# Attention into a dense mixture of experts on one core: joint outputs later in their slot, hi parts of weights and operands on other engines around the last pass, six buffers for raw weights

## The chip, the core and the metric

The kernel runs on one core of a Trainium2 chip. The core has five engines that each work through a queue of their own, in program order, and wait for each other by semaphores: TensorE (PE in the profile, its weight loads PEld), VectorE (DVE), ScalarE (ACT), GpSimd (POOL), and SyncE (SP), which here only issues DMAs. Matmul results land in PSUM, everything else lives in SBUF. The metric is the device time of one launch in microseconds, the median of several runs.

## The reference

The attention part takes q, k, v of shape (4, 8, 576, 64), a memory M_prev (4, 8, 64, 64) with its norm z_prev, and a gate beta per head. The second part runs every token through all four experts.

```python
scores = (q @ k^T) / 8, causal mask; a = softmax(scores); local = a @ v
q_p = where(q > 0, q, exp(q) - 1) + 1
mem_out = (q_p @ M_prev) / (q_p . z_prev + 1e-6)
attn = g * mem_out + (1 - g) * local              # g = sigmoid(beta), per head
x = attn as (2304, 512);  p = probs / sum(probs)
out = sum over e of p[:, e] * (relu(x @ w1[e]) @ w2[e])   # w1 (4,512,1024), w2 (4,1024,512)
```

All inputs and the output are float32.

## The kernel before

**Precision.** Each float32 operand of a large matmul is split into hi and lo: hi is the operand written as fp32r, lo is the operand minus hi. A product is then three matmuls, hi·hi, hi·lo and lo·hi, summed in PSUM. So every weight tile and every activation costs one instruction that writes hi and one that subtracts it to give lo.

**The expert passes.** The 2304 tokens are 18 tiles of 128. Twelve of them form six groups of two tiles (`GROUPS`), six form the last pass (`TAIL`). A phase is one half of one expert: `mm1` makes four blocks of h (`h`, line 848; relu to `hh` on ScalarE, line 857; `hl` on VectorE, line 858), `mm2` multiplies them by w2 (`y`, line 878) and VectorE adds them to `acc` (line 894). A group takes eight phases. Neighbouring groups overlap: phases 0 to 28 hold one or two groups each, phases 25 to 28 only group 5. The last pass is phases 29 to 36 (`tail_phase`). It forms x·w1 by seven block products instead of eight; its operands (`A11`, `S1`, `S2`, `A12`, `S3`, `S4`, `A22`, each 128x768) are made once by `x_ops` from the attention's output `xt`, as eleven pieces: four sums or differences (line 991) and seven `put`s (hi on line 983, lo on line 984). They are dealt out during phases 27 and 28, one after every third part of a phase. Its weights are made by `wt_prep`: four sums of blocks `tsum`, hi `wth` on ScalarE, lo `wtl`. For phase 29 the sums and lo are on VectorE.

**The weights.** `w_dma` loads a raw tile of 128x512 (`stg`, 256 KB) on SP's queue, from a pool of `NSTG` = 4 buffers; `w_prep` makes hi and lo. GpSimd always makes lo (line 247). Hi is on ScalarE (line 244) for w1 until phase 26 and for w2 in the first phases, otherwise on GpSimd (line 246). A new load is issued once a preparation has freed a buffer. w2 of a phase is prepared during that phase's `mm1`, w1 of the next phase during `mm2`; each of the hi and lo buffers for the weights exists once.

**The attention beside it.** The attention is cut into tasks (one pair of heads, two or three query tiles), and tasks into slots. Each step of a task has a slot and a place in it, written in the table `PR` as [slot, place]; steps are sorted by both, and then dealt out between the parts of the expert phases by a running sum of estimated costs (`target`). Twelve tasks are "joint": both heads in one slot, four slots to a task. A joint task's steps on TensorE are `tq`, `tk`, `tp` (transposes of q, k and of phi(q); results split to hi and lo by ScalarE and VectorE, `split_q`, lines 365 to 372), `sp` (scores, line 479), `pt` (transposed probabilities) and `o` (output, lines 551 and 555). `tq`, `tk`, `tp` and `o` share two PSUM buffers ("to"), so each of them waits until the one two places back has been read out.

`j_o`, the joint output, stands at slot +4, place -0.2; the scores `j_qk` of the task that runs in that slot stand at place 0, and the transposes of probabilities at place 7. The read-out of `tp` (`qpa`, `qpb` on VectorE) stands one slot earlier at place 4.5.

```python
ev(i + PR["jo"][0], PR["jo"][1], lambda i=i: j_o(i), 6 * mm(GW) + 4 * mm(P))
act = (kind == "1" or i < START[1]) and i < PH0 - PR["ahead"] and not pool   # PH0 = 29, ahead = 2
```

Of the kernel before, what the change touches and what calls it, by code (L numbers as in the profile page):

```python
# [10 lines left out]
AF = mybir.ActivationFunctionType  # L11
# [11 lines left out]
PR = {  # L23
    "phi1": [-5, 1],
    "phi2": [-5, 7],
    "phi3": [-4, 7],
    "trq": [-3, 6.5],
    "trk": [-4, -0.5],
    "v": -2,
    "trqp": [1, 2.5],  # L30
    "qk": 0,
# [5 lines left out]
    "jn": [1, -0.45],  # L37
    "jp": [2, 7],
    "jlo": 9,
    "jo": [4, -0.2],  # L40
    "wpe": 1500,
    "wvec": 400,
    "frac": 0.97,
# [13 lines left out]
def tile_attention_moe(  # L57
# [13 lines left out]
    nc = tc.nc  # L71
# [38 lines left out]
    START = [g // 2 * NPH + (PR["x"] if g % 2 else 0) for g in range(NG)]  # L110
    PH0 = START[-1] + NPH
# [20 lines left out]
    def f(ap):  # L132
        return ap.bitcast(F32)

    def rows(c):
        return min(P, S - c * P)
# [61 lines left out]
        for kind in "12"  # L198
        for fc in (range(HF) if i < PH0 else (0, 2, 1, 3))
    ]  # L200
    NSTG = 4
    wpos = {"dma": 0, "prep": 0, "due": 0}
    stg = {}

    def w_dma():
        j = wpos["dma"]
        if j >= len(wseq):
            return
        wpos["dma"] += 1
        i, kind, fc = wseq[j]  # L210
        e, hf = halves[i]
        f0 = (hf * HF + fc) * P
        t = sp.tile([P, DM], F32, tag="stg", name=f"stg{j}", bufs=NSTG)
        stg[j] = t
        if kind == "1":
            nc.sync.dma_start(
                out=t.rearrange("p (c f) -> p c f", c=NKD),
                in_=w1[e, :, f0 : f0 + P].rearrange("(c p) f -> p c f", p=P),
            )
        else:  # L220
            nc.sync.dma_start(out=t, in_=w2[e, f0 : f0 + P, :])

    def w_more():

        while wpos["due"]:
            wpos["due"] -= 1
            w_dma()

    def w_prep(i, kind, pool=False):

        act = (kind == "1" or i < START[1]) and i < PH0 - PR["ahead"] and not pool
        j = wpos["prep"]
        if j >= len(wseq) or wseq[j][0] != i or wseq[j][1] != kind:
            return
        w_more()
        wpos["prep"] += 1
        fc = wseq[j][2]
        t = stg.pop(j)
        hi, lo = (w1s if kind == "1" else w2s)[fc]
        if kind == "1":  # L240
            hi = hi.rearrange("p c f -> p (c f)")
            lo = lo.rearrange("p c f -> p (c f)")
        if act:
            nc.scalar.activation(hi, t, AF.Copy)  # L244
        else:
            nc.gpsimd.tensor_scalar(hi, t, 1.0, 1.0, ALU.mult, ALU.mult)  # L246
        nc.gpsimd.tensor_tensor(lo, t, f(hi), ALU.subtract)  # L247
        wpos["due"] += 1
# [566 lines left out]
    def pcol(pieces):  # L815
        b, c = pieces[0]
        return 4 * b + c if c < 4 else 4 * B + b // 2
# [47 lines left out]
    def mm2(i, g, tt, after):  # L865
        e = halves[i][0]
        pieces = GROUPS[g][tt]
        pe = pn[:, pcol(pieces), e : e + 1]
        t0 = (g % 2) * GW + tt * P
        tk = slice(t0, t0 + P)  # L870
        pt = []

        def part(fc):
            if fc == 0:
                pt.append(ps.tile([P, 512], F32, tag="moe", name=f"y{i}_{g}_{tt}", bufs=3))
            wh, wl = w2s[fc]
            for z, (h_, w_) in enumerate(((hh, wh), (hh, wl), (hl, wh))):
                nc.tensor.matmul(  # L878
                    pt[0],
                    lhsT=h_[fc][:, tk],  # L880
                    rhs=w_,
                    start=(fc == 0 and z == 0),
                    stop=(fc == HF - 1 and z == 2),
                )
            if fc == HF - 1:
                fin()
                after()

        def fin():
            if i == START[g]:  # L890
                acc[g, tt] = sp.tile([P, DM], F32, tag="acc", name=f"acc{g}_{tt}", bufs=4)
                nc.vector.tensor_scalar(acc[g, tt], pt[0], pe, None, ALU.mult)
            else:
                nc.vector.scalar_tensor_tensor(  # L894
                    acc[g, tt], pt[0], pe, acc[g, tt], ALU.mult, ALU.add
                )
            if i == START[g] + NPH - 1:
                o0 = 0
                for b, c in pieces:
                    r0, m = b * S + c * P, rows(c)  # L900
                    nc.sync.dma_start(out=out[r0 : r0 + m, :], in_=acc[g, tt][o0 : o0 + m])
                    o0 += m

        return [lambda c=c: part(c) for c in range(HF)]

    def phase_parts(i):
        gs = [g for g in range(NG) if START[g] <= i < START[g] + NPH]
        c0 = min(g % 2 for g in gs) * GW
        cols = slice(c0, c0 + len(gs) * GW)
        out_ = []  # L910
        for fc in range(HF):
            for p_ in mm1(i, fc, cols, lambda: w_prep(i, "2")):
                out_.append((3 * mm(len(gs) * GW), p_))
        if i + 1 in START:
            out_.append((0.0, START.index(i + 1)))
        nt = 2 * len(gs)

        def after():
            if i + 1 == PH0:
                wt_prep(PH0)  # L920
            else:
                for _ in range(HF // nt):
                    w_prep(i + 1, "1")

        for g in gs:
            for tt in range(2):
                for p_ in mm2(i, g, tt, after):
                    out_.append((3 * mm(DM), p_))
        return out_
# [43 lines left out]
    def a_blk(i, k):  # L973
        return xt[:, 2 * k : 2 * k + 2, i * TB : (i + 1) * TB]

    def x_ops():

        X, s_ = tail["x"], tail["s"]
        s3 = tail["r"][:, 0:2]

        def put(n, src, eng):
            hi, lo = X[n]
            nc.scalar.activation(hi, src, AF.Copy)
            eng.tensor_tensor(lo, src, f(hi), ALU.subtract)

        def plain(n, i, k):
            return [lambda: put(n, a_blk(i, k), nc.vector)]

        def summed(n, eng, dst, a, b, op):
            return [  # L990
                lambda: eng.tensor_tensor(dst, a, b, op),
                lambda: put(n, dst, eng),
            ]

        return (
            plain("A11", 0, 0)
            + summed("S1", nc.vector, s_, a_blk(1, 0), a_blk(1, 1), ALU.add)
            + summed("S2", nc.vector, s_, s_, a_blk(0, 0), ALU.subtract)
            + summed("S4", nc.vector, s_, a_blk(0, 1), s_, ALU.subtract)
            + summed("S3", nc.vector, s3, a_blk(0, 0), a_blk(1, 0), ALU.subtract)  # L1000
            + plain("A12", 0, 1)
            + plain("A22", 1, 1)
        )

    def wt_prep(i):

        j = wpos["prep"]
        if j >= len(wseq) or wseq[j][0] != i or wseq[j][1] != "1":
            return
        w_more()  # L1010
        wpos["prep"] += 2
        t1, t2 = stg.pop(j), stg.pop(j + 1)
        hi, lo = tail["w"][wseq[j][2]]
        t = tail["t"]
        b11, b21, b12, b22 = t1[:, 0:GW], t1[:, GW:], t2[:, 0:GW], t2[:, GW:]
        t1 = t1.rearrange("p (n w) -> p n w", w=GW)
        gp = (nc.vector if i == PH0 else nc.gpsimd).tensor_tensor
        gp(t[:, 0], b12, b11, ALU.subtract)
        gp(t[:, 1], b22, t[:, 0], ALU.subtract)
        gp(t[:, 2], b22, b12, ALU.subtract)  # L1020
        gp(t[:, 3], b21, t[:, 1], ALU.subtract)
        nc.scalar.activation(hi[:, 0:2], t1, AF.Copy)
        nc.scalar.activation(hi[:, 2], b22, AF.Copy)
        nc.scalar.activation(hi[:, 3:7], t, AF.Copy)
        gp(lo[:, 0:2], t1, f(hi[:, 0:2]), ALU.subtract)
        nc.vector.tensor_tensor(lo[:, 2], b22, f(hi[:, 2]), ALU.subtract)
        nc.vector.tensor_tensor(lo[:, 3:7], t, f(hi[:, 3:7]), ALU.subtract)
        wpos["due"] += 2
# [86 lines left out]
    def tail_phase(i):  # L1115
        for p in range(2):
            tail_mm1(i, p)
            for _ in range(2):
                w_prep(i, "2")
        for t in range(0, NTL, 2):  # L1120
            tail_mm2(i, (t, t + 1))
            if t < 4:
                wt_prep(i + 1)


    def first_run():
# [20 lines left out]
        for h0, h1 in ((0, 2), (2, 4), (4, 8)):  # L1147
# [3 lines left out]
            if h0 == 0:  # L1151
# [4 lines left out]
                )  # L1156
        for _ in range(NSTG):
            w_dma()
# [310 lines left out]
```

## Time and profile before

| What | Value |
|---|---|
| Median of 3 runs | 1083.83 us (1081.46 to 1086.19) |
| The profiled execution's own time | 1078.98 us |
| Its span, first to last instruction | 1077.2 us |
| TensorE busy | 1011.6 us, 94% |
| VectorE busy | 736.7 us, 68% |
| GpSimd busy | 628.9 us, 58% |
| ScalarE busy | 504.2 us, 47% |
| Mean granted TensorE clock | 0.980 of 2.4 GHz |

TensorE is busy for most of the span, so its idle time and the time in which it runs at less than full clock are what can be read as loss. A row of "windows" cuts the span into stretches and gives the busy time of each engine in each; a row of "waits" gives an engine's idle time by what ended it; the timeline lists instructions with the idle time of their engine just before them in brackets.

### The profile page before, as it was taken

The page shows a single profiled execution, that of the slowest core. Times are in us where ns is not written, and L with a number is a line of the kernel's source. Part 1 is how long each engine was busy: PE and PEld are TensorE (multiplying, and loading weights), DVE is VectorE, ACT ScalarE, POOL GpSimd, SP SyncE. Part 2 cuts the span into 40 slices and gives each one's busy share as a digit, 9 for nine tenths or more (in the row PEclk, how much of TensorE's full clock was granted, in tenths as well). Part 3 has the DMA queues.
Part 4 walks back from the last instruction along what each step waited for, and adds up shares of the span by engine and source line. Part 5 has one row for each costly group of instructions (what it writes and reads, how often), then busy time and mean ns, then how long its engine had stood idle before and what let it go on. Part 6 is the DMA issues. An engine that isn't in the chain of part 4 may idle for free.

```text
span 1077.2 us, 16403 instructions
## 1 busy us (share of the span) xinstructions
PE 1011.6 (94%) x5312; PEld 857.6 (80%) x5312; DVE 736.7 (68%) x1708; ACT 504.2 (47%) x1193; POOL 628.9 (58%) x669
## 2 busy tenths in 40 slices
PE   5887889988999999999999999999978999999998
PEld 3776777777888888878888878778866888999887
DVE  5777767777777788778777878877375555445453
ACT  4666655554555555555555555545223333333231
POOL 4767567555556655565555654647895644555540
PEclk8999899999999999999999999999988999999999
DMA  5557444453445444354444434423434312222211
GB/s 135 132 152 181 118 130 121 120 142 96 109 115 136 103 134 109 97 146 115 116 105 121 121 106 108 115 85 110 146 99 137 88 54 61 62 70 69 78 40 58
DMA packets 205957, 116.87 MB, mean 108 GB/s; under 512 B 100272, under 2 KB 181680, under 8 KB 205872
## 3 DMA queue, kind: packets, MB, share of 16 engines
q1 hardware_dynamic: 205200, 115.56, 39.7%
q8 instruction: 42, 0.69, 0.3%
q14 instruction: 43, 0.35, 0.1%
q10 hardware_dynamic: 672, 0.27, 0.1%
HBM read 100.57 MB, written 4.72 MB: 98 GB/s over the span
## 4 chain that ended last, share of the span: by engine, by line
PE 72%; DVE 12%; POOL 6%; issue 4%; ACT 3%; DMA 2%; SPq 1%; POOLq 0%; DVEq 0%; ACTq 0%
PE h L848 18%; PE y L878 17%; PE yt L1094 12%; PE tc_1X L1043 3%; PE o L722 3%; PE pt L357 3%; PE sp L611 3%; PE tc_0X L1043 3%; POOL w2l L247 3%; DMA stg<-in_moe_w_dram 2%; POOL w1l L247 2%; PE tc_1Y L1043 1%; PE tc_0Y L1043 1%; POOL w2h L246 1%; DVE hl L858 1%
## 5 line engine op out<-in xcount | busy, mean ns | idle before, releaser
L247 POOL TENSOR_TENSOR w1l<-stg,w1h 128x512 fp32r<-128x512 f32 x116 | 153.3, 1328 | 241.1 <-ACT w1h L244 194.7
L247 POOL TENSOR_TENSOR w2l<-stg,w2h 128x512 fp32r<-128x512 f32 x148 | 196.2, 1325 | 18.0 <-ACT w2h L244 6.1
L848 PE MATMUL h<-xh,w1h 128*128 128x512 f32 (+1 forms) x464 | 176.1, 379 | 0.4 <-DVE hl L858 0.4
L848 PE MATMUL h<-xh,w1l 128*128 128x512 f32 (+1 forms) x464 | 165.2, 356 | 1.8 <-POOL w1l L247 1.8
L878 PE MATMUL y<-w2h,hh 128*128 128x512 f32 x384 | 165.1, 430 | 1.6 <-DVE hl L858 1.0
L848 PE MATMUL h<-xl,w1h 128*128 128x512 f32 (+1 forms) x464 | 164.2, 354 | 0.0
L878 PE MATMUL y<-w2l,hh 128*128 128x512 f32 x384 | 155.9, 406 | 7.2 <-POOL w2l L247 5.6
L878 PE MATMUL y<-w2h,hl 128*128 128x512 f32 x384 | 154.9, 403 | 0.2 <-DVE hl L858 0.2
L858 DVE SCALAR_TENSOR_TENSOR hl<-h,hh 128x512 fp32r<-128x512 f32 (+1 forms) x116 | 69.1, 596 | 59.6 <-ACT hh L857 58.6
L857 ACT ACTIVATE hh<-h 128x512 fp32r<-128x512 f32 (+1 forms) x116 | 60.8, 524 | 92.8 <-PE h L848 91.6
L246 POOL TENSOR_SCALAR w2h<-stg 128x512 fp32r<-128x512 f32 x132 | 88.1, 667 | 19.9 <-DMA stg<-in_moe_w_dram 12.7
L848 PEld LDWEIGHTS h<-xh,w1l 128*128 128x128 f32 x464 | 87.5, 189 | 15.1 <-POOL w1l L247 2.2
L894 DVE SCALAR_TENSOR_TENSOR acc<-y,pn,acc 128x512 f32<-128x512 f32 x84 | 62.8, 748 | 51.7 <-PE y L878 50.9
L848 PEld LDWEIGHTS h<-xh,w1h 128*128 128x128 f32 x464 | 87.8, 189 | 9.3 <-DVE hl L858 0.6
L848 PEld LDWEIGHTS h<-xl,w1h 128*128 128x128 f32 x464 | 88.2, 190 | 7.7
L878 PEld LDWEIGHTS y<-w2l,hh 128*128 128x128 f32 x384 | 74.9, 195 | 21.9 <-POOL w2l L247 12.1
L658 ACT ACTIVATE pth<-pt 128x384 fp32r<-128x384 f32 (+3 forms) x128 | 50.4, 421 | 85.4 <-PE pt L357 84.7
L878 PEld LDWEIGHTS y<-w2h,hl 128*128 128x128 f32 x384 | 74.5, 194 | 17.1 <-DVE hl L858 0.5
L878 PEld LDWEIGHTS y<-w2h,hh 128*128 128x128 f32 x384 | 74.8, 195 | 14.3 <-POOL w2h L246 1.8
L1107 DVE SCALAR_TENSOR_TENSOR xt<-yt,pn,xt 128x512 f32<-128x512 f32 x42 | 31.5, 751 | 61.1 <-PE yt L1094 61.1
L357 PE MATMUL pt<-ident,s 128*128 128x128 f32 (+1 forms) x376 | 62.0, 276 | 10.3 <-DVE ptl L660 8.3
L357 PEld LDWEIGHTS pt<-ident,s 128*128 128x128 f32 (+1 forms) x376 | 45.4, 139 | 29.6 <-issue 10.9
(297 smaller groups left out, 2440.6 us busy)
## 6 DMA issues: line engine op xcount, KB each, us to landing
stg<-in_moe_w_dram SPq DMA_DIRECT2D x296, 256.0 KB, 2.8
natall<-in_k_dram SPq DMA_DIRECT2D x34, 128.0 KB, 2.7
natall<-in_v_dram SPq DMA_DIRECT2D x32, 128.0 KB, 3.0
natall<-in_q_dram SPq DMA_DIRECT2D x60, 64.0 KB, 2.6
out_dram<-acc SPq DMA_DIRECT2D x12, 256.0 KB, 2.1
kha<-kha SPq DMA_DIRECT2D x16, 128.0 KB, 2.4
khb<-khb SPq DMA_DIRECT2D x16, 128.0 KB, 2.3
natall<-in_k_dram SPq DMA_DIRECT2D x28, 64.0 KB, 2.6
```

What stands on the lines that cost most here:

```text
L246: nc.gpsimd.tensor_scalar(hi, t, 1.0, 1.0, ALU.mult, ALU.mult)
L247: nc.gpsimd.tensor_tensor(lo, t, f(hi), ALU.subtract)
L357: nc.tensor.transpose(dst, src, ident[0:n, 0:n])
L611: nc.tensor.matmul(pt[:, 0 : b_ - a], lhsT=q_, rhs=qk[k_][:, a:b_], start=y == 0, stop=y == len(pairs) - 1,)
L658: nc.scalar.activation(dh, src, AF.Copy)
L848: nc.tensor.matmul(pt[0][:, cols], lhsT=w_[:, c], rhs=x_[:, c, cols], start=(c == 0 and z == 0), stop=(c == NKD - 1 and z == 2),)
L857: nc.scalar.activation(h_, pt[0][:, cols], AF.Relu)
L858: nc.vector.scalar_tensor_tensor(l_, pt[0][:, cols], 0.0, f(h_), ALU.max, ALU.subtract)
L878: nc.tensor.matmul(pt[0], lhsT=h_[fc][:, tk], rhs=w_, start=(fc == 0 and z == 0), stop=(fc == HF - 1 and z == 2),)
L894: nc.vector.scalar_tensor_tensor(acc[g, tt], pt[0], pe, acc[g, tt], ALU.mult, ALU.add)
L1043: nc.tensor.matmul(bank[b][:, 0:TB], lhsT=w_[:, n, cs], rhs=x_[:, c], start=first and c == 0 and z == 0, stop=c == 1 and z == 2, skip_grou ...
L1094: nc.tensor.matmul(o, lhsT=h_[fc][:, tk], rhs=w_, start=(z == 0 and fc == p and y == 0), stop=(z == 1 and fc == p + 2 and y == 2),)
```

## The change

Five edits:

1. The joint output `j_o` moves from place -0.2 to place 3 of its slot.
2. Raw weights have six buffers instead of four.
3. For phases 27 and 28, hi of w1 and w2 is made by ScalarE and no longer by GpSimd.
4. In phase 28 the first `wt_prep` for phase 29 is called after the first block of the first token tile of `mm2`, not after its last; the second follows at the end of the first tile, not of the second.
5. In `x_ops`, hi of the last pass's operands is copied by VectorE (`tensor_copy`) and no longer by ScalarE.

```diff
-    "jo": [4, -0.2],
+    "jo": [4, 3],
...
-    NSTG = 4
+    NSTG = 6
...
-        act = (kind == "1" or i < START[1]) and i < PH0 - PR["ahead"] and not pool
+        act = (kind == "1" or i < START[1] or PH0 - PR["ahead"] <= i < PH0) and not pool
...
+            if fc == 0 and i + 1 == PH0 and tt == 0:
+                wt_prep(PH0)
             if fc == HF - 1:
                 fin()
...
         def put(n, src, eng):
             hi, lo = X[n]
-            nc.scalar.activation(hi, src, AF.Copy)
+            eng.tensor_copy(hi, src)
             eng.tensor_tensor(lo, src, f(hi), ALU.subtract)
```

TensorE's queue around the third joint output (`o` is the output, `sp` the scores of the next task, `y` the experts' second product). Before:

```order
L878 MATMUL y_0_0_1334<-w2h_123,hl_111 128x512
L551 MATMUL o_1342<-qpa_86,ms_0_509 128x256
L555 MATMUL o_1342<-pth_99,v_983 128x256
...
L555 MATMUL o_1342<-ptl_100,v_983 128x128
L878 MATMUL y_0_0_1334<-w2h_125,hh_108 128x512
...
L878 MATMUL y_0_0_1334<-w2h_127,hl_113 128x512
L479 MATMUL sp_1364<-kha_96,qa_91 128x256
...
L878 MATMUL y_0_0_1334<-w2h_129,hh_110 128x512
```

And with the change:

```order
L878 MATMUL y_0_0_1338<-w2h_123,hl_111 128x512
L479 MATMUL sp_1348<-kha_96,qa_91 128x256
...
L878 MATMUL y_0_0_1338<-w2h_125,hh_108 128x512
...
L878 MATMUL y_0_0_1338<-w2h_127,hl_113 128x512
L551 MATMUL o_1365<-qpa_86,ms_0_513 128x256
L555 MATMUL o_1365<-pth_99,v_987 128x256
...
L555 MATMUL o_1365<-ptl_100,v_987 128x128
L878 MATMUL y_0_0_1338<-w2h_129,hh_110 128x512
```

The ten matmuls of `o` now stand behind the four of `sp` and six of `y`. Over the twelve joint tasks they move behind the four of `sp` and, in four tasks, three matmuls of the experts, in seven, six, and in one, none.

VectorE's queue in the same task keeps its order: the read-out of `tp` (`qpa`, `qpb`), then the scores' masking (`s`), and some instructions later the sum that reads `o` (L582):

```order
L369 SCALAR_TENSOR_TENSOR qpa_94<-tp_1307,qpa_94 64x256
L372 SCALAR_TENSOR_TENSOR qpb_95<-tp_1307,qpb_95 64x256
L858 SCALAR_TENSOR_TENSOR hl_114<-h_3_1312,hh_110 128x256
L484 ISA s_1346,st_1347<-sp_1348,mask 128x256
...
L369 SCALAR_TENSOR_TENSOR qa_83<-tq_1324,qa_83 64x256
L372 SCALAR_TENSOR_TENSOR qb_84<-tq_1324,qb_84 64x256
L896 SCALAR_TENSOR_TENSOR acc_0_677<-y_0_0_1338,pn,acc_0_677 128x512
L541 TENSOR_TENSOR ptl_102<-pt_1397,pth_101 128x2x128
L582 TENSOR_TENSOR xr<-o_1365,otmp_1376 64x256 x2
```

Only `acc` and the read-out of `tq` (`qa`, `qb`) have changed places there.

VectorE's queue at the end of phase 28 (`hl` belongs to `mm1`, `tsum` and `wtl` to the weights of phase 29, `acc` to the token tile). Before:

```order
L984 TENSOR_TENSOR A22l<-xt,A22h 128x768
L858 SCALAR_TENSOR_TENSOR hl_113<-h_2_8868,hh_109 128x256
L858 SCALAR_TENSOR_TENSOR hl_114<-h_3_8887,hh_110 128x256
L894 SCALAR_TENSOR_TENSOR acc_0_7444<-y_5_0_8906,pn,acc_0_7444 128x512
L1018 TENSOR_TENSOR tsum<-stg_8883,stg_8862 128x256
```

And with the change:

```order
L986 CAST A22h<-xt 128x768
L987 TENSOR_TENSOR A22l<-xt,A22h 128x768
L858 SCALAR_TENSOR_TENSOR hl_113<-h_2_8872,hh_109 128x256
L858 SCALAR_TENSOR_TENSOR hl_114<-h_3_8891,hh_110 128x256
L1021 TENSOR_TENSOR tsum<-stg_8845,stg_8824 128x256
...
L1030 TENSOR_TENSOR wtl_8690<-tsum,wth_8689 128x1024
L896 SCALAR_TENSOR_TENSOR acc_0_7448<-y_5_0_8910,pn,acc_0_7448 128x512
```

Seven casts of 128x768 come in, and the seven instructions of the first `wt_prep` stand ahead of `acc`. GpSimd's queue loses the sixteen hi instructions of phases 27 and 28 and keeps the sixteen subtractions; ScalarE's queue loses the seven hi instructions of the operands and gains those sixteen, one behind each relu and four after each `mm2`.

## Rows read from the trace of the kernel before

**Rows 1.** Windows: stretch, length, busy per engine, clock, DMA share, GB/s.

```profile
54.00:108.00 54.00, 42.88 (x278) 37.67 (x277) 40.29 (x101) 32.96 (x91) 38.35 (x43) 0.96 0.63 166
500.00:600.00 100.00, 99.68 (x517) 83.25 (x517) 80.05 (x196) 53.96 (x127) 54.67 (x53) 1.00 0.45 118
800.00:835.00 35.00, 28.82 (x144) 24.26 (x143) 21.67 (x32) 12.53 (x23) 23.88 (x23) 0.90 0.41 126
835.00:880.00 45.00, 44.98 (x223) 39.98 (x222) 23.17 (x36) 15.15 (x29) 22.47 (x26) 1.00 0.22 65
```

**Rows 2.** Waits of TensorE: in total, times, longest.

```profile
PE o L551 <- DVE qpb L372: 22.6, 10, 3.6
```

**Rows 3.** Timeline of TensorE: the longest and shortest wait of the ten.

```profile
106.76 0.55 PE L551 MATMUL o<-qpa,ms 128*128 128x256 f32 x1 [3.57 <-DVE qpb L372]
...
209.52 0.35 PE L551 MATMUL o<-qpa,ms 128*128 128x256 f32 x1 [0.60 <-DVE qpb L372]
```

**Rows 4.** Windows behind two of the waits, and one whole task.

```profile
66.00:72.00 6.00, 4.34 (x20) 3.79 (x21) 2.23 (x6) 1.91 (x4) 1.46 (x2) 0.75 0.20 54
85.00:91.00 6.00, 4.28 (x26) 3.60 (x27) 2.90 (x10) 3.45 (x8) 1.99 (x2) 1.00 0.99 231
106.76:125.95 19.19, 15.87 (x99) 14.46 (x100) 14.26 (x37) 12.07 (x32) 12.55 (x12) 0.92 0.46 130
```

**Rows 5.** Timeline: TensorE's pace at full clock, behind the third wait.

```profile
111.22 0.28 PE L479 MATMUL sp<-kl,qz 128*128 128x256 f32 x1
...
111.34 0.39 PE L878 MATMUL y<-w2h,hh 128*128 128x512 f32 x1
...
111.57 0.40 PE L878 MATMUL y<-w2l,hh 128*128 128x512 f32 x1
```

**Rows 6.** Timeline of VectorE and ScalarE around the third wait.

```profile
106.18 0.43 DVE L372 SCALAR_TENSOR_TENSOR qpb<-tp,qpb 64x256 fp32r<-64x256 f32 x1
...
109.16 0.77 ACT L569 ACTIVATE otmp<-o 64x256 f32<-64x256 f32 x2 [5.90 <-PE o L555]
...
111.54 0.43 DVE L484 CUSTOM_DVE_ANT_0 s<-sp,mask 128x256 f32<-128x256 f32 x1 [4.47 <-PE sp L479]
...
114.23 0.85 DVE L582 TENSOR_TENSOR xr<-o,otmp 64x256 f32<-64x256 f32 x2
```

**Rows 7.** Timeline of TensorE: starts of phase 27, phase 28, last pass.

```profile
780.22 0.28 PE L848 MATMUL h<-xh,w1h 128*128 128x256 f32 x1
...
801.11 0.28 PE L848 MATMUL h<-xh,w1h 128*128 128x256 f32 x1
...
820.75 0.34 PE L1043 MATMUL tc_0X<-A11h,wth 128*128 128x384 f32 x1
...
824.72 0.44 PE L1043 MATMUL tc_0X<-S2h,wth 128*128 128x384 f32 x1 [1.72 <-ACT trow L1054]
```

**Rows 8.** Timeline of GpSimd: first, one contended, last of 32 instructions.

```profile
776.82 0.62 POOL L246 TENSOR_SCALAR w1h<-stg 128x512 fp32r<-128x512 f32 x1
...
785.95 1.32 POOL L246 TENSOR_SCALAR w2h<-stg 128x512 fp32r<-128x512 f32 x1
...
813.92 1.27 POOL L247 TENSOR_TENSOR w2l<-stg,w2h 128x512 fp32r<-128x512 f32 x1
```

**Rows 9.** Timeline of VectorE: two operands' lo, phase 27's last hl.

```profile
785.06 1.74 DVE L984 TENSOR_TENSOR S1l<-xsum,S1h 128x768 fp32r<-128x768 f32 x1 [0.58 <-ACT S1h L983]
...
788.99 1.03 DVE L984 TENSOR_TENSOR S2l<-xsum,S2h 128x768 fp32r<-128x768 f32 x1 [0.57 <-ACT S2h L983]
789.94 0.41 DVE L858 SCALAR_TENSOR_TENSOR hl<-h,hh 128x256 fp32r<-128x256 f32 x1
```

**Rows 10.** Lines 654 and 244: ns minimum, median, maximum, first and last start.

```profile
L654 DVE TENSOR_SCALAR s<-s,st x80: 419/520/1709, 268.5 to 755.3; 128x384 f32<-128x384 f32 x32, 128x512 f32<-128x512 f32 x32, 128x576 f32<-128x576 f32 x16
...
L244 ACT ACTIVATE w1h<-stg x104: 613/622/635, 50.8 to 764.8; 128x512 fp32r<-128x512 f32 x104
```

**Rows 11.** Timeline of SyncE at the start: three loads of raw weights.

```profile
19.82 6.08 SPq L221 DMA_DIRECT2D stg<-in_moe_w_dram  x3
```

## The prediction

> **What bounds the kernel now.** I read the windows first. In the middle of the span (500 to 600 us) and in the last pass (from 835 us) TensorE is busy 99.7% and 100% at a clock of 1.00 [rows 1]. Nothing that the change touches can shorten those stretches. Two others fall short: the joint tasks up to about 270 us (clock 0.96 and 42.9 of 54 us busy in the first of their windows) and the passage into the last pass (28.8 of 35 us, clock 0.90) [rows 1]. So the question is what ends TensorE's idle time in these two, which the waits and then the timeline answer.
>
> In the joint tasks it is one wait: ten of the twelve joint outputs wait for VectorE's read-out of `tp`, 22.6 us in total [rows 2], between 0.60 and 3.57 us each [rows 3]. It is the PSUM buffer that `o` waits for, since `tp` holds it. A second loss follows: behind four of the waits the clock falls to half for some 3 us. The window behind the first shows 0.75 over 6 us, a loss of 1.5 us; behind a wait of 2.4 us the clock stays at 1.00 [rows 4]. Four such windows make about 6 us.
>
> The third wait shows why VectorE is late. It ends `qpb` at 106.6 and TensorE goes on at 106.76; then VectorE itself waits 4.47 us, until 111.54, for the scores, which stand in TensorE's queue behind `o` [rows 6]. The two engines stop each other in turn. In that task VectorE is busy 14.3 of 19.2 us [rows 4].
>
> At the passage the bound is GpSimd. Phases 27 and 28 run from 780.2 to 801.1 and to 820.75, some 20 us each [rows 7]. At the pace of full clock (0.12 us for 256 columns, 0.23 us for 512 [rows 5]) 48 and 24 matmuls would take 48 x 0.12 + 24 x 0.23 = 11.3 us. GpSimd meanwhile works without a gap from 776.8 to 815.2, sixteen pairs of hi and lo [rows 8]. VectorE adds to it: an instruction that takes 0.62 us takes 1.32 us while VectorE subtracts in SBUF [rows 8], and VectorE's own subtraction takes 1.74 us instead of 1.03 [rows 9]. Each holds up the other.
>
> **Edit 1, the joint output.** It moves behind the four score matmuls (0.48 us) and mostly three or six expert matmuls (0.69 or 1.38 us). If VectorE finished no earlier than now, the ten waits would shrink by just this, task by task: 11.9 of 22.6 us go and 10.7 stay, the longest 2.8 us. That is the lower bound, 12 us, with the clock no better. The upper bound is all of the waits and the clock, 22.6 + 6 = 29 us. Between them it hangs on VectorE. With the scores first, its 4.47 us of idle time go, and it reaches the next `qpb` some 3 to 4 us sooner; but at 14.3 us of work per task it then fills some 90% of a task that would last about 15.5 us (TensorE's own work there, 15.9 us busy less 1.6 us for the lost clock, is 14.3 us too). So neither engine leaves much room, small waits will remain, and I take 22 us, nearer the upper end because of the row on the 4.47 us. What is behind the moved instruction: `otmp` on ScalarE (0.77 us for the pair) and, on VectorE, the sum on line 582, which today starts 4.3 us after `otmp` is done [rows 6]. That distance is its cover; if it goes, VectorE waits in its place (fourth rival).
>
> **Edits 3 to 5, the passage.** Sixteen hi instructions leave GpSimd, the first at 776.8. Its sixteen subtractions stay at 1.27 us [rows 8], 20.3 us. The present 38.4 us exceed the sixteen pairs at 0.62 + 1.27 us and gaps of 0.07 us by 38.4 - 31.5 = 6.9 us; that is what VectorE's eleven sums and subtractions cost GpSimd, 0.63 us each. They stay. The seven casts are new. No row shows them; the nearest is line 654, one operand in SBUF: 0.42 us at least for up to 576 columns, 0.52 median, 1.71 at most [rows 10]. For 768 columns I take 0.55 us alone, and up to 1.7 us when held up. At GpSimd's share of 0.6 they cost it 7 x 0.35 = 2.5 us. Its last subtraction then ends at 776.8 + 20.3 + 6.9 + 2.5 = 806.5 us; one block and the second token tile still follow on TensorE, some 3.4 us: 810 us.
>
> VectorE comes out nearly the same. Its last `hl` of phase 27 ends at 790.35 now [rows 9]. The two waits for ScalarE in front of it (0.58 and 0.57 us [rows 9]) go, three casts come: about 791.5. TensorE needs it at 780.2 + 5.8 for `mm1` + 2.5 for three blocks of `mm2` = 788.5, waits 3 us and ends phase 27 near 795. From 791.5 to its last `hl` of phase 28 VectorE has four casts (2.2 us), six sums and subtractions of 1.03 us (6.2), four `hl` (1.6) and two `acc` of 512 columns, which I estimate at 0.75 us from the 0.41 us of 256 (1.5), and for the ten in SBUF 0.35 us of hold-up each, the mean of none and of 1.74 - 1.03 (3.5): 806.5 us. TensorE then ends near 810. Both chains meet there. ScalarE is no bound: it is busy 12.5 of 35 us there [rows 1], and sixteen instructions of 0.62 us [rows 10], 10 us, replace its seven longer ones.
>
> Edit 4 takes the first `wt_prep` from behind `acc` to behind the last `hl`. Its sums then no longer wait for the first token tile. The third product of the last pass waits for `trow`, which ScalarE writes behind the second `wt_prep`'s hi, 1.7 us today [rows 7]. I leave it 2.5 us: the product that starts at 824.7 now [rows 7] starts near 814.3. The passage gains 10.5 us. Its bounds: 6 us when each of VectorE's eighteen instructions is held up as the 1.74 us row is, 16 us when the casts pass beside GpSimd unhindered and the clock stays up.
>
> The Trainium skill, "SBUF — State Buffer" (section "SBUF: two separate sides"), says that VectorE and GpSimd share a port pair by an exclusive lock that the first holds for its whole instruction, and names fp32 copies in SBUF as takers. The rows on 1.32 and 1.74 us agree that one blocks the other. By that rule edit 5 puts seven more holders of the lock beside the engine that sets the pace. Where the casts always meet a subtraction, this is the third rival.
>
> **Edit 2, six buffers.** Two more loads stand at the start ahead of M_prev and v on SyncE's queue, which delays these by about 2 us. Behind them SyncE waits 6 us over three raw weights for GpSimd [rows 11], and it still waits for the same three preparations, so q, k and v of the first task leave when they do now. I cost it at nothing, between -2 and +2 us.
>
> **The sum.** 22 + 10.5 = 32.5 us off the profiled execution's own 1078.98 us (span 1077.2) is 1046.5 us. The median of the runs stands 4.85 us above that execution, so the median should be about 1051 us.
>
> **The rivals.**
> First, everything goes: no joint wait remains, and VectorE and GpSimd pass each other at the passage, 29 + 16 = 45 us, 1039 us. Against it stands VectorE's 90%. Chance 0.06.
> Second, VectorE becomes the bound of the joint tasks and the waits shrink only by the work that they were moved past: 12 + 10.5 us, 1061 us. For it speaks 14.3 of 15.5 us; against it that the middle of the span runs TensorE at 99.7% with VectorE at 80% [rows 1]. Chance 0.14.
> Third, the casts: each waits for a subtraction and then holds up the next one, VectorE's eighteen instructions at 1.5 us each (27 us), eight `hl` and three `acc` (5.5) take from 781 to 813.5 us, and the passage gains 6 us: 22 + 6 = 28 us, 1056 us. For it speak the two held-up rows, against it that the unhindered ones are as many [rows 9]. Chance 0.14.
> Fourth, slower: `o` comes so late that VectorE, which works in order, reaches the sum on line 582 before `otmp` is written, and stands there. Between `qpb` and that sum VectorE has one `hl` (0.41 us [rows 9]) and what it does from 111.54 to 114.23 [rows 6], 3.1 us in all; `o` and `otmp` took 3.2 us from 106.76 on. The two are level, so it decides only when TensorE reaches `o` well after `qpb`. At 3.5 us per task the joint tasks would keep their present waits, moved to VectorE, and add the delay of about 1.5 us in each of twelve: +18 - 10.5, 1091 us. Chance 0.04.
> Fifth, no change to speak of: waits and passage re-form elsewhere. Chance 0.02.
>
> **How the numbers follow.** The forecast, 1051 us, has 0.60; its own range is 1044 to 1058. The range of eight in ten reaches from the first rival to beyond the second, 1038 to 1066 us. Half a per cent (5.4 us) is about what a measurement of this kernel can tell from no change; its own runs lie 4.7 us apart. Faster by more: 0.60 + 0.06 + 0.14 + 0.14 = 0.94. Within: 0.02. Slower: 0.04.
>
> **What would show it.** In the waits of TensorE, `o` behind `qpb` should stand below 8 us, and no window behind a joint output should show a clock near 0.75. VectorE should no longer wait for `sp` for 4 us. From the first `h` of phase 27 to the third product of the last pass it should be about 34 us instead of 44.5, with GpSimd's subtractions back to back and ScalarE's hi never waited for. The casts of 768 columns should lie between 0.5 and 1.2 us. The forecast is wrong in the joint tasks if the `o` waits stay above 11 us, and at the passage if phases 27 and 28 still take over 17 us each.

## The result, and the profile after

The changed kernel takes 1068.18 us (median of 4 runs, 1067.04 to 1071.60) against 1084.74 us (4 runs, 1081.46 to 1086.19): ratio 0.9857, 95% interval 0.9823 to 0.9890. It is some 16 us faster, half of what was forecast, and 2 us outside the range. Both terms of the sum came out too large.

The profiled execution took 1067.27 us (span 1065.5 us). TensorE starts phase 9, behind the joint tasks, at 260.63 us (before 268.18); the third product of the last pass starts at 812.29 (before 824.72). That is 7.5 us from the joint tasks and 4.9 us from there to the third product, 0.7 of which are lost again by the end. Since the profiled execution of before ran 5 to 6 us under its median, the parts are better sized by medians, further down.

The windows that answer to [rows 1], the passage now from 785 us on:

```profile
54.00:108.00 54.00, 46.41 (x283) 40.30 (x281) 43.32 (x98) 32.82 (x91) 37.96 (x42) 0.91 0.62 158
500.00:600.00 100.00, 99.76 (x524) 84.14 (x525) 76.47 (x188) 52.40 (x122) 54.37 (x54) 1.00 0.42 110
785.00:820.00 35.00, 27.55 (x132) 24.18 (x133) 31.14 (x40) 10.63 (x21) 21.85 (x17) 0.85 0.40 125
```

TensorE's busy time in the first window rose from 42.88 to 46.41 us, but the clock fell from 0.96 to 0.91, so part of it is the same work at 1.2 GHz. In the passage VectorE is busy 31.14 of 35 us, GpSimd only 21.85: the prediction had GpSimd as the bound there before, and both ending together after the change.

The waits of TensorE from 50 to 300 us (columns as in [rows 2]):

```profile
PE o L551 <- DVE qpb L372: 9.1, 6, 2.8
PE y L878 <- DVE hl L858: 4.9, 4, 2.4
PE pt L357 <- DVE s L520: 2.0, 2, 1.2
```

The waits of the joint output fell from 22.6 [rows 2] to 9.1 us, as far as the lower bound said (10.7 stay). The lower bound had VectorE finishing no earlier than before. Others grew: 4.9 us for `hl`, where 1.2 us stood before. Both are waits for VectorE's queue, and the clock falls behind them. TensorE around the second joint output, then what VectorE and GpSimd did up to it, then the window behind it (the granted clock stands behind GpSimd's busy time):

```profile
86.17 0.39 PE L878 MATMUL y<-w2h,hl 128*128 128x512 f32 x1
88.81 0.55 PE L551 MATMUL o<-qpa,ms 128*128 128x256 f32 x1 [2.25 <-DVE qpb L372]
```

```profile
85.01 0.59 DVE L511 SCALAR_TENSOR_TENSOR st<-st,ebp 128x2 f32<-128x2 f32 x1
85.63 0.17 DVE L514 RECIPROCAL st<-st 128x2 f32<-128x2 f32 x1
85.83 1.63 DVE L520 TENSOR_SCALAR s<-s,st 128x128 f32<-128x128 f32 x2
87.38 0.41 DVE L858 SCALAR_TENSOR_TENSOR hl<-h,hh 128x256 fp32r<-128x256 f32 x1
87.81 0.42 DVE L369 SCALAR_TENSOR_TENSOR qpa<-tp,qpa 64x256 fp32r<-64x256 f32 x1
88.24 0.43 DVE L372 SCALAR_TENSOR_TENSOR qpb<-tp,qpb 64x256 fp32r<-64x256 f32 x1
```

```profile
85.53 0.62 POOL L352 TENSOR_TENSOR qp<-qp,rn 128x256 f32<-128x256 f32 x1
86.11 1.27 POOL L247 TENSOR_TENSOR w2l<-stg,w2h 128x512 fp32r<-128x512 f32 x1
```

```profile
88.00:92.00 4.00, 3.19 (x13) 3.03 (x14) 2.27 (x8) 0.76 (x2) 0.00 (x0) 0.60 1.09 249
```

VectorE has no idle time here; it is late by its own queue. Ahead of `hl`, `qpa` and `qpb` stands the scaling of the joint scores (L511 to L520, `j_sum` and `j_norm`), and its two instructions took 1.63 us: VectorE's row ends where GpSimd's instruction ends, at 87.4. The same pair takes 0.48 us elsewhere (below). Of the twelve pairs in front of a joint task's `qpb`, three took 1.2 us or more before and six do now (1.28 to 2.27 us). Behind this wait TensorE's granted clock is 0.60 in the mean of 4 us, so part of them runs at 1.2 GHz.

At the passage, VectorE's seven casts (columns: count, min/median/max ns, starts):

```profile
L986 DVE CAST A11h<-xt x1: 1173/1173/1173, 773.1 to 773.1; 128x768 fp32r<-128x768 f32 x1
L986 DVE CAST S1h<-xsum x1: 1311/1311/1311, 777.6 to 777.6; 128x768 fp32r<-128x768 f32 x1
...
L986 DVE CAST S3h<-trow x1: 551/551/551, 793.0 to 793.0; 128x768 fp32r<-128x768 f32 x1
L986 DVE CAST A12h<-xt x1: 1661/1661/1661, 794.8 to 794.8; 128x768 fp32r<-128x768 f32 x1
```

They sum to 8.3 us. The one at 793.0, when GpSimd stood idle (its next row begins at 794.78 after 5.42 us of idle time), took 0.55 us, as estimated. The others took 0.98 to 1.66. The waits of TensorE from 768 us on:

```profile
783.18 0.50 PE L878 MATMUL y<-w2h,hl 128*128 128x512 f32 x1 [2.58 <-DVE hl L858]
786.67 0.80 PE L878 MATMUL y<-w2h,hl 128*128 128x512 f32 x1 [2.52 <-DVE hl L858]
798.86 0.50 PE L878 MATMUL y<-w2h,hh 128*128 128x512 f32 x1 [0.78 <-DVE hl L858]
802.37 0.50 PE L878 MATMUL y<-w2h,hl 128*128 128x512 f32 x1 [1.41 <-DVE hl L858]
812.29 0.62 PE L1046 MATMUL tc_0X<-S2h,wth 128*128 128x384 f32 x1 [3.55 <-ACT trow L1057]
```

Where TensorE waited for GpSimd's `w2l` before, here in total, it now waits for VectorE's `hl`, and for the third product 3.55 us instead of 1.72 [rows 7].

```profile
PE y L878 <- POOL w2l L247: 5.6, 8, 1.4
```

### The profile page after: what moved, and what is told of

It is laid out like the page before. It is cut to its first block, busy times and chain, and to the rows that moved or that the text cites. A ratio compares the mean times of both kernels' runs of the same rounds, so it can differ in the third digit from the quotient of the medians.

```text
span 1065.5 us, 16437 instructions
## 1 busy us (share of the span) xinstructions
PE 1008.9 (95%) x5312; PEld 858.2 (81%) x5312; DVE 757.5 (71%) x1715; ACT 506.0 (47%) x1202; POOL 618.4 (58%) x653
## 3 DMA queue, kind: packets, MB, share of 16 engines
q1 hardware_dynamic: 205200, 115.56, 39.6%
## 5 line engine op out<-in xcount | busy, mean ns | idle before, releaser
L878 PE MATMUL y<-w2l,hh 128*128 128x512 f32 x384 | 153.3, 399 | 1.3 <-POOL w2l L247 1.3
L246 POOL TENSOR_SCALAR w2h<-stg 128x512 fp32r<-128x512 f32 x124 | 81.3, 656 | 12.3 <-PE yt L1097 7.2
```

The lines of the kernel that those rows point to most:

```text
L878: nc.tensor.matmul(pt[0], lhsT=h_[fc][:, tk], rhs=w_, start=(fc == 0 and z == 0), stop=(fc == HF - 1 and z == 2),)
```

## The experiments

Times are medians against the runs of the kernel before on the same chip, as ratio with its 95% interval. Places in the program are from the profile of each: "phase 9" is its first `h` (before 268.18, changed 260.63), "passage" the time from phase 27's first `h` to the third product (before 44.5, changed 40.0 us).

**One part alone.** Edit 1 alone (`"jo": [4, -0.2]` to `[4, 3]` in the kernel before), and the changed kernel without it:

> Edit 1 alone: the joint output in mid-slot, all else as before. In the two profiles phase 9 starts 7.5 us earlier with the whole change, and nothing shifts from there to phase 27. Theory A (the joint part of the change was worth 8 us, because VectorE's lateness is the bound and the wait only moves from the joint output to the second projection's read of hl): phase 9 starts 7 to 8.5 us earlier than before, the shift stays constant to the end, the span is 7 to 9 us shorter, ratio about 0.992. Rival B (edit 1 was worth the forecast 22 us, and the six buffers or the moved weights' hi spoil it in the first phases, where phases 2 and 3 start 2 us later): phase 9 starts 12 us or more earlier, ratio 0.985 or less, and phases 2 and 3 start no later than before.

> The changed kernel with the joint output put back to where it was before; edits 2 to 5 stay. Theory A (joint and passage are independent; the passage gives 4.5 us net): phases up to 27 start within 0.7 us of before, the third product of the last pass starts 4 to 5.5 us earlier, the span is 3 to 5 us shorter, ratio about 0.996. Rival B (the passage was worth the forecast 10 us, and an earlier arrival after the joint gain spoiled it): the third product starts 8 us or more earlier.

Edit 1 alone: 1071.33 us, ratio 0.9893 [0.9878, 0.9908], phase 9 at 258.97, passage 44.6 us; the joint output's waits 8.5 us. Without edit 1: 1079.07 us, 0.9962 [0.9947, 0.9977], phase 9 at 273.20, passage 39.6 us. So by the medians edit 1 is worth 11.7 us and edits 2 to 5 together 3.9 us; the sum, 15.6 us, is the whole change within its interval. They don't disturb each other, which is the first theory of both; but its figures were missed. Edit 1 alone gave 9.2 us up to phase 9, where 7 to 8.5 were expected, and 11.7 by the medians. Without edit 1 the ratio came as expected, but phase 9 starts 5 us later than in the profile of before, not within 0.7 us, most likely because the profiled execution of before ran 4 us under its kernel's median in this set. Phases 2 and 3 start later than there with edit 1 alone (four buffers) and without it (six) alike, so this can't be laid to edit 2.

**The passage, edits 5 and 2 undone**, apart and together:

```
 def put(n, src, eng):
-    eng.tensor_copy(hi, src)
+    nc.scalar.activation(hi, src, AF.Copy)     # edit 5 undone
-    NSTG = 6
+    NSTG = 4                                    # edit 2 undone
```

> The changed kernel with the hi of the last pass's operands cast on ScalarE again (edit 5 undone), all else as changed. In the changed profile the seven casts on VectorE take 0.55 us once and 1.0 to 1.7 us the other six times, 8.3 us in all, and VectorE's hl is what TensorE waits for in phase 27 (7.3 us in four waits). Theory A (VectorE's chain is the bound of the passage and the casts lengthen it by their own time and by what they hold GpSimd up): phases 27 and 28 together get 3 to 7 us shorter than in the changed kernel (33.9 us there), the y waits for hl fall to less than half, the span is 3 to 6 us shorter than the changed kernel's. Rival B (ScalarE, which now writes the weights' hi as well, becomes the bound, its instructions of 0.6 us coming late before each subtraction): no gain, or 1 to 3 us longer. Rival C (GpSimd's eight pairs of 1.3 us subtractions per projection set the pace whoever casts): within 1 us of the changed kernel.

> The changed kernel with four buffers for raw weights instead of six (edit 2 undone). Theory A (edit 2 was worth nothing): every phase starts within 0.5 us of the changed kernel, the span too. Rival B (six buffers delay q, k and v of the first tasks and cost the 1.7 to 2.2 us by which phases 2 and 3 start later): phases 2 and 3 start 1.5 to 2 us earlier than in the changed kernel. Rival C (the passage needs the six buffers: with four, raw weights land later once ScalarE writes their hi): phase 27 or 28 starts 1 us or more later.

> The changed kernel with edits 2 and 5 undone: four buffers, hi of the operands on ScalarE; edits 1, 3 and 4 stay. From phase 27's first h to the third product of the last pass the changed kernel takes 40.0 us, with four buffers 37.6, with the casts on ScalarE 35.5. In the changed kernel GpSimd splits weights of a later phase at 804.4 to 809.8, beside VectorE's work on wt, whose instructions there take 2.31, 0.84 and 1.37 us against 1.23, 0.42 and 0.43 with four buffers. Theory A (two separate losses: the casts on VectorE, and GpSimd's early work that six buffers let in): they add up, the stretch takes 32.5 to 34 us, the wait for the third product falls from 3.8 us to below 2.2, the span is 2 to 3.5 us shorter than with the casts alone undone, ratio about 0.979. Rival B (the two loosen the same wait): 35 to 36 us, no gain over the casts alone undone.

| Casts on | Buffers | Median, us | Ratio | Passage, us |
|---|---|---|---|---|
| VectorE | six (changed) | 1068.18 | 0.9857 [0.9823, 0.9890] | 40.0 |
| ScalarE | six | 1062.23 | 0.9809 [0.9793, 0.9826] | 35.5 |
| VectorE | four | 1062.91 | 0.9822 [0.9801, 0.9844] | 37.6 |
| ScalarE | four | 1058.81 | 0.9756 [0.9742, 0.9771] | 33.4 |

In the passage the casts cost 4.5 us with six buffers and 4.2 with four, the six buffers 2.4 and 2.1 us: two separate losses that add up. By the medians the six buffers cost more, 5.3 us (the two intervals overlap) and, with the casts on ScalarE, 3.4 us; 0.7 us of it lies behind the third product (252.3 and 252.4 us from there to the end with four buffers, 253.0 and 253.2 with six), and the rest is not located. With both undone the passage takes 33.4 us, 11 us less than before: edits 3 and 4 alone bring what the forecast gave to edits 3 to 5 with the casts counted in. Of the first run theory A held: with the casts on ScalarE TensorE's waits for `hl` from 768 us on fall from 7.3 us in four to this one, here with four buffers:

```profile
PE y L878 <- DVE hl L858: 0.7, 1, 0.7
```

Its rivals B and C (ScalarE or GpSimd as the bound) fell. Of the second run nothing that was expected came: the buffers are not worth nothing (A), phases 2 and 3 start 1.2 and 0.1 us earlier with four, not 1.5 to 2 (B), and phase 27 starts earlier, not later (C). In the third the two losses add up, theory A.

What the buffers do shows in VectorE's rows before the third product, first in the changed kernel, then with four buffers:

```profile
804.63 0.84 DVE L1029 TENSOR_TENSOR wtl<-stg,wth 128x256 fp32r<-128x256 f32 x1
805.39 2.31 DVE L1030 TENSOR_TENSOR wtl<-tsum,wth 128x1024 fp32r<-128x1024 f32 x1
...
808.73 1.37 DVE L1022 TENSOR_TENSOR tsum<-stg,tsum 128x256 f32<-128x256 f32 x1
```

```profile
802.64 0.42 DVE L1029 TENSOR_TENSOR wtl<-stg,wth 128x256 fp32r<-128x256 f32 x1
803.25 1.23 DVE L1030 TENSOR_TENSOR wtl<-tsum,wth 128x1024 fp32r<-128x1024 f32 x1 [0.19 <-ACT wth L1027]
...
805.50 0.43 DVE L1022 TENSOR_TENSOR tsum<-stg,tsum 128x256 f32<-128x256 f32 x1
```

and in GpSimd's of the same two kernels:

```profile
804.41 0.78 POOL L246 TENSOR_SCALAR w2h<-stg 128x512 fp32r<-128x512 f32 x1 [3.25 <-PE y L878]
805.28 1.34 POOL L247 TENSOR_TENSOR w2l<-stg,w2h 128x512 fp32r<-128x512 f32 x1
806.59 1.59 POOL L246 TENSOR_SCALAR w2h<-stg 128x512 fp32r<-128x512 f32 x1
808.27 1.55 POOL L247 TENSOR_TENSOR w2l<-stg,w2h 128x512 fp32r<-128x512 f32 x1
```

```profile
808.40 1.04 POOL L246 TENSOR_SCALAR w2h<-stg 128x512 fp32r<-128x512 f32 x1 [9.21 <-DMA stg<-in_moe_w_dram]
```

With six buffers the raw weights of the next expert are there when TensorE's last `y` frees the buffer for their hi, at 804.4 us, and GpSimd splits them at once, beside the very instructions of VectorE that the third product waits for. With four they land behind them, and GpSimd stands idle 9.2 us. The third product waits 1.71 us with four buffers and 3.55 with six. The earlier transfer made the later work collide.

**Edit 4 undone** (the two lines that call `wt_prep(PH0)` taken out):

> The changed kernel with edit 4 undone: the first preparation of wt again behind the acc of the first token tile. In the changed kernel its instructions run on VectorE from 802.57 to 807.6 us while TensorE does the first tile's second projection, and the acc comes behind them. Theory A (edit 4 takes VectorE's wt work out of the chain to the third product): the third product comes 2 to 4.5 us later than in the changed kernel, the span is 2 to 4 us longer. Rival B (the acc that now stands behind it costs as much, since TensorE's second tile needs its buffer): within 1 us.

1069.22 us, ratio 0.9852 [0.9836, 0.9869]; the third product 0.9 us later than in the changed kernel, the span 1.2 us longer, the passage 41.4 us, 1.4 us longer. Theory A's 2 to 4 us are not there: edit 4 is worth some 1 us in the profile of this kernel, and the medians, 1.0 us apart, lie within each other's intervals. Edit 3 was not undone by itself.

**The joint tasks: is it VectorE's load?** The scaling moved to ScalarE, with the joint output at either place, and the scaling done twice:

```
-    nc.vector.tensor_scalar(s.s3[:, hd], s.s3[:, hd], r[:, hd : hd + 1], None, ALU.mult)
+    nc.scalar.activation(s.s3[:, hd], s.s3[:, hd], AF.Copy, scale=r[:, hd : hd + 1])
```
```
     nc.vector.tensor_scalar(s.s3[:, hd], s.s3[:, hd], r[:, hd : hd + 1], None, ALU.mult)
+    nc.vector.tensor_scalar(s.s3[:, hd], s.s3[:, hd], 1.0, None, ALU.mult)
```

> The changed kernel with the scaling of the joint scores (two instructions of 0.65 us per slot, 34 of them on VectorE between 108 and 260 us, 20.8 us) on ScalarE instead of VectorE. Theory A (in the joint tasks the length of VectorE's work sets when qpb and hl come, and TensorE's remaining waits of 18 us between 50 and 300 us are that): some 2.6 us per task leave VectorE, the waits fall below 9 us, phase 9 starts 5 to 10 us earlier than in the changed kernel, ratio about 0.977. Rival B (VectorE is busy only 78% there and waits for ScalarE 15 us itself, so the round of waits among the three engines is the bound and ScalarE's added work lengthens it): phase 9 within 2 us of the changed kernel, or later.

> As the run before, and the joint output back where it was before (edit 1 undone). It tells how much of the 22.6 us of joint output waits is place and how much is VectorE's length. Theory A (length): phase 9 starts 6 us or more earlier than with edit 1 undone alone (273.2 us there), the joint output's waits for qpb fall from 24.4 us to below 16. Rival B (place: the wait of the scores behind the joint output is what makes VectorE late, so lighter work only lengthens VectorE's idle time of 4.5 us for the scores): phase 9 within 2 us of 273, waits above 21 us.

> The changed kernel with each scaling of the joint scores followed by one more instruction of the same size on VectorE (times 1.0): 46 instructions more in the joint tasks. At the mean of 0.65 us that the first ones take there it is 30 us of VectorE work more, 14 us at their undisturbed 0.30 us. Theory A (VectorE's chain is the bound, so that each us of work ahead of hl and qpb is a us of time): phase 9 starts 14 to 30 us later than in the changed kernel. Rival B (VectorE has 20% to spare and mutual waits are the bound): 8 us later or less.

On ScalarE: 1092.92 us, 1.0071 [1.0046, 1.0096], phase 9 at 287.10; with the joint output back, 1111.49 us, 1.0241 [1.0226, 1.0257], phase 9 at 304.29. This is 25 us the wrong way against the changed kernel, and 32 against the one without edit 1: theory A, the sheer length of VectorE's work, fell in that form; rival B's longer time came in the first run, while in the second it fell too. From 108 to 260 us VectorE now waits 18.1 us for `hh`, and ScalarE for VectorE (first run):

```profile
ACT s L520 <- DVE st L514: 42.8, 16, 5.5
```

ScalarE stands 42.8 us in front of the scaling, until VectorE has the reciprocal, and `qpa`, `qpb` and `hh` stand behind it in its queue. The run says that the place in a queue counts; it does not say what VectorE's length is worth. The doubled scaling does: one execution of 1095.78 us, phase 9 at 288.36, 27.7 us later than in the changed kernel. The trace has 48 instructions more, not the 46 of the expectation, of 33.3 us in all. So nearly every microsecond put in front of `hl` and `qpb` comes back as time (theory A): VectorE's chain sets the pace there, though it is busy only 71.46 of 92 us from 108 to 200 us. A part of the 27.7 us is the clock, 0.87 in that stretch against 0.98 in the changed kernel, and it is a single execution.

**The order in VectorE's queue.** One number: `"jn": [1, -0.45]` to `[1, 4.6]`, which puts the scaling, with the sum and the reciprocal in front of it (lines 511 to 520), behind `qpa` and `qpb`; on edits 1, 3 and 4 (four buffers, casts on ScalarE), and alone on the kernel before.

> Edits 1, 3 and 4 with four buffers and the casts on ScalarE, and one number more: the scaling of the joint scores stands behind qpa and qpb in VectorE's queue instead of ahead of them. In the changed kernel this scaling, two instructions that take 0.30 us each undisturbed, takes 2.27, 1.63, 1.62 and 1.28 us just ahead of the late qpb (those at 66, 86, 123.5 and 221.5 us) with GpSimd at work beside it. The run that put the scaling on ScalarE did not settle it, since ScalarE then stood 42.8 us waiting for the reciprocals. Theory A (what still makes the joint output wait is that held-up scaling in front of qpb): the joint output's waits fall from 8.4 us to below 3, phase 9 starts 4 to 8 us earlier than with edits 1, 3 and 4 alone (258.6 us there), ratio about 0.970. Rival B (VectorE's whole length per task is the bound, its order is not): waits move to pt for s and to y for hl, phase 9 within 2 us. Rival C (the transposes now wait for the later scaling): phase 9 later by 2 us or more.

> The kernel before with that one number alone: the scaling of the joint scores behind qpa and qpb, the joint output where it was. Theory A (the scaling in front of qpb is part of all ten waits of the joint output): its waits fall from 22.6 us to 8 to 14, phase 9 starts 7 to 12 us earlier than before, much as edit 1 alone does (8 to 9.2 us). Rival B (the place of the joint output decides, since VectorE comes to qpb late because it stood 25.6 us waiting for the scores behind the last joint output): waits stay above 18 us, phase 9 within 3 us of before.

With edits 1, 3 and 4: 1047.76 us (4 runs, 1046.12 to 1049.29), ratio 0.9663 [0.9644, 0.9681], phase 9 at 246.97, 11.7 us earlier than the same kernel without it. Alone on the kernel before: 1064.32 us, 0.9810 [0.9791, 0.9829], phase 9 at 254.77. Theory A of both held, and by more than expected: that number alone is worth at least as much as the whole change, 20.5 us by the medians. The waits of TensorE from 50 to 300 us, first with edits 1, 3 and 4, then alone:

```profile
PE pt L357 <- DVE s L520: 3.7, 4, 1.2
...
PE o L551 <- DVE qpb L372: 1.1, 2, 0.8
PE y L878 <- DVE hl L858: 0.8, 2, 0.6
```

```profile
PE o L551 <- DVE qpb L372: 7.7, 9, 2.2
PE pt L357 <- DVE s L520: 3.1, 4, 1.1
```

VectorE at the second joint output of the first of the two, where the rows of the changed kernel above had the scaling in front:

```profile
81.41 0.42 DVE L369 SCALAR_TENSOR_TENSOR qpa<-tp,qpa 64x256 fp32r<-64x256 f32 x1
81.84 0.43 DVE L372 SCALAR_TENSOR_TENSOR qpb<-tp,qpb 64x256 fp32r<-64x256 f32 x1
82.30 0.42 DVE L858 SCALAR_TENSOR_TENSOR hl<-h,hh 128x256 fp32r<-128x256 f32 x1
82.64 0.15 DVE L511 SCALAR_TENSOR_TENSOR st<-st,ebp 128x2 f32<-128x2 f32 x1
82.82 0.17 DVE L514 RECIPROCAL st<-st 128x2 f32<-128x2 f32 x1
83.02 0.48 DVE L520 TENSOR_SCALAR s<-s,st 128x128 f32<-128x128 f32 x2
```

The joint output waits 1.1 us in all, and the scaling, late as it is now, costs `pt` 3.7 us instead of 2.0. The pair is still held up in five of the twelve tasks (1.26 to 2.32 us), but nothing that TensorE waits for soon stands behind it. What no run parts is how much of the 11.7 us is GpSimd's hold-up and how much the bare place: in front of the twelve `qpb` lines 511 to 520 took 21.3 us without that number, and twelve times the undisturbed 0.80 us of the rows above would be 9.6 us. This is the fastest kernel of the study.

## Why the prediction was wrong

The mechanisms that came were named, as rivals; both terms of the sum were sized by the wrong case. What happened is the second and the third rival at once: 12 us from the joint tasks (edit 1 alone measured 11.7) and 6 from the passage (6.9 with four buffers). Each rival stood with the other term at its forecast. Together they make 1066 us, the last value of the range, and the loss by edit 2 carried the time past it. The third rival's 6 us does not follow from its own figures either: a last `hl` at 813.5 instead of 806.5 us leaves 3.5 of the 10.5 us. With 3.5 the two make 1068 us; that this meets the measured time is luck, since VectorE's eighteen instructions took 25.1 us and not 27, and the loss by edit 2 is not in it.

**Edit 1, forecast 22 us, measured 11.7.** The step that failed: "With the scores first, its 4.47 us of idle time go, and it reaches the next `qpb` some 3 to 4 us sooner". The first half held: VectorE's waits for `sp`, 25.6 us in nine before, are no longer among its waits. The second did not. From the first joint task to the first task behind them `qpb` comes every 17.4 us instead of 18.1, so 0.7 us sooner, where 15.5 were forecast. VectorE's waits from 50 to 300 us, two of before and one of the changed kernel:

```profile
DVE s L484 <- PE sp L479: 25.6, 9, 4.5
...
DVE ptl L541 <- ACT pth L540: 1.4, 4, 0.6
```

```profile
DVE ptl L541 <- ACT pth L540: 12.7, 8, 3.7
```

Two things took the time that the scores gave back. One is this wait for ScalarE's `pth`; why it grew was not tested by itself (with the scaling moved it is 4.7 us). The other is the scaling ahead of `qpb`, which I left out of the path; in front of the twelve `qpb` it took 15.0 us instead of 10.8. That its place costs time is shown by the runs that moved it. Both kernels' profiles show the rows: the pair in front of the third `qpb` of before, with which [rows 6] begin, had taken 1.62 us already.

```profile
102.69 0.86 DVE L511 SCALAR_TENSOR_TENSOR st<-st,ebp 128x2 f32<-128x2 f32 x1
103.58 0.17 DVE L514 RECIPROCAL st<-st 128x2 f32<-128x2 f32 x1
103.79 1.62 DVE L520 TENSOR_SCALAR s<-s,st 128x128 f32<-128x128 f32 x2
```

I asked what VectorE waits for behind `qpb`, where the rows in front of it held the answer. With the scaling out of the way, phase 9 starts 21.2 us earlier than before, close to the 22 us that I had forecast for a queue in which it still stood; that the figures agree confirms nothing. The clock gave nothing back either: from 50 to 250 us it is 0.96, before 0.97. The 6 us that the upper bound counted for it would have needed waits behind which it stays up. A wait of 2.40 us had been such a one [rows 4], but 0.60 stands behind a wait of 2.25.

**Edits 3 to 5, forecast 10.5 us, measured 6.9 in the passage.** That is with four buffers; with edit 2 it is 4.5, and 3.9 by the medians without edit 1. Edits 3 and 4 brought 11 us, the casts took 4.2 of them. The step that failed is the price of the casts, "for 768 columns I take 0.55 us alone", with 0.35 us of hold-up each: 0.9 us. They took 1.18 in the mean, and four of the seven subtractions behind them took 1.9 us, where the other three took 0.96. VectorE's last `hl` of phase 27 ended 14.4 us after the phase's start, where 11.3 were forecast (780.2 to 791.5), and behind a wait of 2.5 us for it TensorE went on at 1.2 GHz, as the window shows:

```profile
787.00:790.00 3.00, 3.00 (x8) 2.32 (x8) 2.97 (x4) 0.00 (x0) 2.36 (x2) 0.50 0.45 145
```
The two chains did not meet: GpSimd stood idle for 5.42 us up to 794.78, VectorE came late. With edit 5 alone undone the passage takes 35.5 us, 1.4 more than the forecast (814.3 - 780.2 = 34.1), which had counted the casts in. The third rival had the cause right and thought it less likely because unhindered rows were as many; but of the seven casts six fell beside GpSimd's subtractions. The Trainium skill, "SBUF — State Buffer" (section "SBUF: two separate sides"), has it that of a GpSimd instruction and a VectorE instruction that takes the second port too, as an fp32 copy in SBUF does, whichever starts first keeps the shared port pair for its whole instruction. The rows of 0.55 against 0.98 to 1.66 us agree.

**Edit 2, forecast 0, between -2 and +2.** No run shows a cost at the start (phase 3 at 95.3 us with six buffers, 95.2 with four). But it lost 2.1 to 2.4 us at the other end of the weights' queue, before the third product, and 3.4 to 5.3 us by the medians: I looked for it only where the first loads stand. It is also where "I leave it 2.5 us" for the third product's wait failed, with 3.55 us measured and 1.7 to 1.8 with four buffers.

**What was right.** VectorE no longer waits for `sp`; the two parts add up; ScalarE was no bound at the passage even with the weights' hi and the casts together (33.4 us); the sum on line 582 did not stop VectorE in the joint tasks, so nothing of the fourth rival came. Of the signs that were named, the others failed: 9.1 us of joint waits and not below 8, a clock of 0.60 behind one, casts of up to 1.66 us and not 1.2, a passage of 40.0 us and not 34.

## What to carry to other kernels

When one engine waits for a result of another, read the late engine's queue backwards from the late instruction, through rows without idle time too, and ask of each row whether it has to stand in front; here one number that let the needed read-out pass a scaling was worth at least as much as the five edits. When work is moved onto an engine, price it by the rows in which its neighbour on the same memory port is busy, not by the undisturbed one, if the neighbour is busy there all the time. When more buffers let work start earlier, look at what that work then stands beside. Two rivals in different stages can both come true, so price their sum as well.

## What the runs showed of the hardware

Short instructions in SBUF on VectorE can take several times as long beside GpSimd. In the changed kernel's joint tasks the pair of scalings of 128 columns took 0.48 us with nothing of GpSimd beside it, 0.60 to 0.75 beside GpSimd instructions of up to 0.62 us, and up to 2.27 us beside its subtractions of some 1.3 us; each scaling that was held up ended 0.08 to 0.09 us after the end of a GpSimd instruction. `qpa`, `qpb` and the `hl` of 256 columns, which read PSUM, took 0.41 to 0.43 us there, beside GpSimd's work too. And how long TensorE waited last does not by itself tell the clock behind it: 2.40 us left it at 1.00 in one profile, 2.25 us at the same joint output were followed by 0.60 in the other.
